# The fifth product of a channel block, taken for two blocks at once on half of the partitions each

## Chip, core and metric

The kernel runs on one core of a Trainium2 chip. The metric is the device time of one execution in microseconds (us); less is better. The core's engines are called as the profile calls them: PE is TensorE's matmul, PEld its weight load, DVE is VectorE, ACT is ScalarE, POOL is GpSimd, and SP issues DMAs. Products are summed in PSUM, of which a bank holds 128 partitions x 512 fp32.

## The reference

```
x, u: (8, 4096, 192)   w_tok1: (4096, 256)   w_tok2: (256, 4096)   w_ch1: (192, 1536)   w_ch2: (1536, 192)
x  = causal 7-tap convolution of x along the sequence; taps are the softmax of each of 8 heads' weights
h  = relu(x^T @ w_tok1) @ w_tok2          # along the sequence, per batch
u  = x + h^T
out = u + relu(u @ w_ch1) @ w_ch2         # along the channels
```

The weights come as float64 and are decoded on the core into a high and a low part.

## The kernel before

The batches are done in groups of one, one, two, two and two. A tile is 512 rows of the sequence of one batch; there are 64 tiles. While the channel part of a group runs on TensorE, VectorE and ScalarE convolve and mix the next group in the background.

A full-precision product is made of products in float32r, of which one pass takes the high part of a number and another pass the rest. `transposed()` turns a tile of u (512 rows x 192 channels) so that channels lie on partitions, and leaves three tiles of 128 x 512: `a`, the high part of channels 0 to 127; `b`, their low part; and `c`, in whose one half lie the high parts of channels 128 to 191 and in whose other half the low parts (for the first batch of a group the high parts are on partitions 0 to 63, for the second on 64 to 127).

Channel product 1 (`channel1`, with `channel1_mm`) makes 12 blocks of 128 hidden channels for each tile. A block is five products, each with 128 partitions and 512 columns, summed into one `ps_x` bank: `ah` with `a`, `al` with `a`, `ah` with `b`, `ch` with `c`, `cl` with `c`. `ch` and `cl` are the high and low parts of the last 64 rows of w_ch1, each standing twice, on the lower and on the upper 64 partitions; they are the two halves of the tile `w_c`. ScalarE then writes the relu's high part `hh`, and VectorE the rest `hl`, both from the same bank. `ps_x` has four banks, which the blocks take in turn; the transposes and mixing product 2 (`mix2`) take them too. The very first tile goes through `first_channel1`, which writes one fp32 tile in place of `hh` and `hl`.

Channel product 2 (`channel2`, lines 921 and 922) makes four sums of 12 x 2 products from `hh` and `hl`. Per tile the order on TensorE is: channel product 1, (for the last batch of a group) mixing product 2 of the next tile, one half of channel product 2, (likewise) the transposes of the next tile, the other half of channel product 2.

The order of the background work is set when the program is built, by a planner (`Background`) with two clocks, `pe` and `dve`, in ns. `bg.fg(pe, dve)` moves on TensorE's clock by the cost of a foreground step, puts background items into the queues until VectorE's clock is 600 ns past TensorE's, and then adds the step's own VectorE cost. For a block of channel product 1 the call is

```
bg.fg(1080, 700)
```

and the block's `hh` and `hl` are issued behind it, so what `fg` has put into the queues stands ahead of them. A taps item is two VectorE instructions (L624).

Of the kernel before, what the change touches and what calls it, by code (L numbers as in the profile page):

```python
# [8 lines left out]
F32 = mybir.dt.float32  # L9
F32R = mybir.dt.float32r  # L10
U32 = mybir.dt.uint32
AF = mybir.ActivationFunctionType
ALU = mybir.AluOpType
# [96 lines left out]
def conv_mixer_kernel(ctx: ExitStack, tc: tile.TileContext, x, weight, w_tok1, w_tok2, w_ch1, w_ch2, out):  # L110
    nc = tc.nc
# [5 lines left out]
    P = 128  # L117
    NJ = S // P
    KC = JT // P
    NF = FF // P  # L120
    D2 = D - P
    TJ = 4
    NT = NJ // TJ
    TT = TJ * P
# [5 lines left out]
    def f32(ap):  # L130
        return ap.bitcast(F32)
# [5 lines left out]
    ps_x = ctx.enter_context(tc.tile_pool(name="ps_x", bufs=4, space=bass.MemoryType.PSUM))  # L137
    ps_c2 = ctx.enter_context(tc.tile_pool(name="ps_c2", bufs=2, space=bass.MemoryType.PSUM))
    ps_a = ctx.enter_context(tc.tile_pool(name="ps_a", bufs=1, space=bass.MemoryType.PSUM))
    bg = Background()  # L140

    w1 = {n: const.tile([P, FF], F32R, name=f"w1_{n}") for n in ("ah", "al")}
# [682 lines left out]

    def transposed(gi, u):

        nb = len(GROUPS[gi])
        abc = [{n: (sp if i else up).tile([P, TT], F32R, name=f"{n}{i}") for n in ("a", "b", "c")} for i in range(nb)]

        rest = up.tile([P, TJ, 2, D2], F32, name="rest")
        for i in range(2):
            nc.scalar.copy(out=rest[:, :, i, :], in_=u[:, :, min(i, nb - 1), P:D])  # L833

        def cols(j, c):
            return u[:, j, c, 0:P] if c < nb else rest[:, j].rearrange("p b d -> p (b d)")

        for c in range(nb + 1):
            ps = ps_x.tile([P, TT], F32, name="ps_x")
            for j in range(TJ):  # L840
                nc.tensor.transpose(out=ps[:, j * P:(j + 1) * P], in_=cols(j, c), identity=ident)  # L841
            bg.fg(440, 600 if c < nb else 600 * nb)
            if c < nb:
                t = abc[c]
                nc.scalar.copy(out=t["a"], in_=ps)  # L845
                nc.vector.tensor_tensor(out=t["b"], in0=ps, in1=f32(t["a"]), op=ALU.subtract)
            else:
                for i in range(nb):
                    t = abc[i]["c"]
                    hs = slice(0, D2) if i == 0 else slice(D2, 2 * D2)  # L850
                    ls = slice(D2, 2 * D2) if i == 0 else slice(0, D2)
                    nc.scalar.copy(out=t[hs], in_=ps[hs])
                    nc.vector.tensor_tensor(out=t[ls], in0=ps[hs], in1=f32(t[hs]), op=ALU.subtract)  # L853
        return abc

    t2s_of(0)
    up = ctx.enter_context(tc.tile_pool(name="up", bufs=1))
    first = {}
# [12 lines left out]
    def first_transposed():  # L871
        first["abc"] = transposed(0, first["u"][1])

    def channel1_mm(t, f):
        fs = slice(f * P, (f + 1) * P)
        ps = ps_x.tile([P, TT], F32, name="ps_x")
        prods = (("ah", "a"), ("al", "a"), ("ah", "b"), ("ch", "c"), ("cl", "c"))
        for n, (w, v) in enumerate(prods):
            nc.tensor.matmul(out=ps, lhsT=w1[w][:, fs], rhs=t[v], start=n == 0, stop=n == len(prods) - 1)  # L879
        return ps  # L880


    def first_channel1(fs):
        for f in fs:
            ps = channel1_mm(first["abc"][0], f)
            bg.fg(1080, 0)
            nc.scalar.activation(out=first["h"][:, f], in_=ps, func=AF.Relu)

    def first_channel2(u, osb, js):
        for j in js:  # L890
# [9 lines left out]
    def channel1(t):  # L900
        h = {}
        for f0 in range(0, NF, NF // 3):
            for n in ("hh", "hl"):
                part = hp.tile([P, NF // 3, TT], F32R, name=f"{n}{f0}")
                for f in range(NF // 3):
                    h[n, f0 + f] = part[:, f]
        for f in range(NF):
            ps = channel1_mm(t, f)
            bg.fg(1080, 700)
            nc.scalar.activation(out=h["hh", f], in_=ps, func=AF.Relu)  # L910
            nc.vector.scalar_tensor_tensor(  # L911
                out=h["hl", f], in0=ps, scalar=0.0, in1=f32(h["hh", f]), op0=ALU.max, op1=ALU.subtract
            )
        return h

    def channel2(i, h, u, osb, js):
# [33 lines left out]
    def first_done():  # L950
# [8 lines left out]
    stage1_first(  # L959
        pe, p0, pd, first_late, first_load, first_next, first_done,  # L960
        [first_mix, first_transposed] + [lambda fs=fs: first_channel1(fs) for fs in thirds],
    )
    pd_ctx.close()
# [65 lines left out]
    for gi, bs in enumerate(GROUPS):  # L1029
        nb = len(bs)  # L1030
# [9 lines left out]
        if gi == 0:  # L1040
            u, abc = first["u"][1], first["abc"]
            loaded = first["next"]
        for q in range(NT):
            nxt = (gi, q + 1) if q + 1 < NT else (gi + 1, 0)
            for i, b in enumerate(bs):
                turn = i == nb - 1 and nxt[0] < len(GROUPS)
                run_ahead(gi)
                if turn and nxt[0] != gi:
                    starts[nxt[0]][1]()
                    if gi == 0:  # L1050
                        cp = cp or conv_pool()
                        t2s_ctx.close()
                        sp = ctx.enter_context(tc.tile_pool(name="sp1", bufs=1, reuse_waits="tile"))
# [3 lines left out]
                if ahead:  # L1057
                    h = channel1(abc[i])
                    run_ahead(gi)
                    osb = hp.tile([P, TJ, D], F32, name="osb")  # L1060
                else:
                    osb = first["osb"]
                    first_channel2(u, osb, half[0])
# [7 lines left out]
                if turn:  # L1071
                    abc = transposed(nxt[0], loaded[1])
# [50 lines left out]
```

## Time and profile before

| what | value |
|---|---|
| median of 3 runs | 2143.77 us (2142.07 to 2144.6) |
| profiled execution | 2145.54 us |
| its span, first to last instruction | 2143.6 us |
| granted TensorE clock | 0.998 |
| PE, PEld, DVE, ACT busy | 2108.9, 1948.3, 1369.2, 733.3 us |
| products of line 879 | 3840 = 64 tiles x 12 blocks x 5 |

Busy times of an engine are the union of its instructions' times. A matmul's time runs from its start to a modelled end and overlaps the next one's; what a matmul costs in a row of them is the distance between starts. In a timeline the columns are start in us, duration in us, engine, line, operation, written tile and read tiles, shape and count, and in brackets how long the engine was idle before it and what released it.

### The profile page before, as it was taken

What the parts mean: (1) busy time and instruction counts of PE and PEld (TensorE: products, weight loads), DVE (VectorE), ACT (ScalarE), POOL (GpSimd) and SP (SyncE); (2) the same over time, 40 slices, a digit from 0 to 9 for tenths busy, and PEclk for the clock granted to TensorE, in tenths of its full rate; (3) what the DMA queues carried; (4) which work ended last, traced back from release to release, by engine and by line L of the source; (5) the groups of instructions that cost most, each with busy time, mean ns of one, the idle gap of its engine ahead of it and who ended that gap; (6) DMA issues with size and microseconds to landing.
All of it is one profiled execution on the core that took longest, in us unless ns stands there. A gap on an engine that the chain in (4) does not pass through costs nothing.

```text
span 2143.6 us, 29665 instructions
## 1 busy us (share of the span) xinstructions
PE 2108.9 (98%) x12202; PEld 1948.3 (91%) x12202; DVE 1369.2 (64%) x2564; ACT 733.3 (34%) x1231; POOL 74.3 (3%) x134
## 2 busy tenths in 40 slices
PE   5999999999999999999999999999999999999999
PEld 5889999999999999999999999999999999999998
DVE  5789979888788986964445884444444444444443
ACT  3455544343433333333223332233223232223222
POOL 1100000000000000000000000000000000000000
PEclk9999999999999999999999999999999999999999
DMA  9835544554534634341112432111111111111100
GB/s 315 264 121 178 172 150 140 179 178 144 174 110 151 197 126 124 97 149 33 47 50 85 144 118 70 42 50 50 50 30 47 46 34 50 49 43 50 50 16 15
DMA packets 159175, 221.83 MB, mean 103 GB/s; under 512 B 106166, under 2 KB 116406, under 8 KB 154432
## 3 DMA queue, kind: packets, MB, share of 16 engines
q1 hardware_dynamic: 148240, 157.36, 24.3%
q0 software_dynamic: 10800, 62.58, 7.3%
q8 instruction: 96, 1.57, 0.3%
q14 instruction: 39, 0.32, 0.0%
HBM read 147.03 MB, written 71.30 MB: 102 GB/s over the span
## 4 chain that ended last, share of the span: by engine, by line
PE 94%; DVE 2%; DMA 1%; ACT 1%; issue 1%; POOL 0%; SPq 0%; ACTq 0%
PE ps_x L879 38%; PE ps_c L921 28%; PE ps_c L922 12%; PE ps_x L841 2%; PE ps_a L712 2%; PE ps_x L819 2%; PE ps_x L817 2%; PE ps_a L714 2%; PE ps_x L818 2%; PE ps_a L713 2%; PE ps_a L708 1%; PE ps_a L428 1%; PE ps_x L814 1%; DVE hl L911 1%; PE ps_x L495 1%
## 5 line engine op out<-in xcount | busy, mean ns | idle before, releaser
L921 PE MATMUL ps_c<-w,hh 128*128 128x384 f32 x3024 | 869.9, 360 | 0.0
L922 PE MATMUL ps_c<-w,hl 128*128 128x192 f32 x3024 | 757.3, 250 | 0.0
L910 ACT ACTIVATE hh<-ps_x 128x512 fp32r<-128x512 f32 x756 | 448.7, 598 | 880.8 <-PE ps_x L879 880.0
L911 DVE SCALAR_TENSOR_TENSOR hl<-ps_x,hh 128x512 fp32r<-128x512 f32 x756 | 511.9, 689 | 278.2 <-ACT hh L910 277.0
L922 PEld LDWEIGHTS ps_c<-w,hl 128*128 128x128 f32 x3024 | 578.8, 191 | 1.0
L921 PEld LDWEIGHTS ps_c<-w,hh 128*128 128x128 f32 x3024 | 567.8, 188 | 1.0
L879 PE MATMUL ps_x<-c,w_c 128*128 128x512 f32 x1536 | 474.3, 390 | 0.1
L624 DVE SCALAR_TENSOR_TENSOR xc<-raw,cw,xc 128x384 f32<-128x384 f32 (+1 forms) x768 | 386.0, 562 | 16.8 <-ACT xc L622 16.2
L879 PEld LDWEIGHTS ps_x<-c,w_c 128*128 128x128 f32 x1536 | 288.9, 188 | 61.3 <-DVE c L853 0.8
L925 DVE TENSOR_TENSOR osb<-ps_c,u 128x192 f32<-128x192 f32 x252 | 89.8, 356 | 370.1 <-PE ps_c L922 369.4
L879 PE MATMUL ps_x<-a,w_ah 128*128 128x512 f32 x768 | 303.3, 395 | 2.0 <-DVE hl L911 2.0
L879 PE MATMUL ps_x<-b,w_ah 128*128 128x512 f32 x768 | 299.8, 390 | 0.0
L879 PE MATMUL ps_x<-a,w_al 128*128 128x512 f32 x768 | 299.7, 390 | 0.0
L879 PEld LDWEIGHTS ps_x<-a,w_ah 128*128 128x128 f32 x768 | 144.6, 188 | 32.6 <-DVE hl L911 5.8
L879 PEld LDWEIGHTS ps_x<-b,w_ah 128*128 128x128 f32 x768 | 144.5, 188 | 30.4
L879 PEld LDWEIGHTS ps_x<-a,w_al 128*128 128x128 f32 x768 | 144.8, 188 | 26.6
L845 ACT CAST a<-ps_x 128x512 fp32r<-128x512 f32 x64 | 35.2, 588 | 190.7 <-PE ps_x L841 190.6
L822 DVE TENSOR_TENSOR u<-ps_x,u 128x384 f32<-128x384 f32 (+1 forms) x160 | 75.3, 472 | 32.7 <-PE ps_x L819 29.3
L926 DVE TENSOR_TENSOR osb<-ps_c,osb 128x192 f32<-128x192 f32 x252 | 90.1, 358 | 8.7
L933 POOL DMA_DIRECT2D out_dram<-osb x63 | 35.8, 568 | 1604.8 <-DVE osb L926 1583.7
L833 ACT COPY rest<-u 128x256 f32<-128x256 f32 x80 | 28.5, 403 | 119.8 <-DVE u L822 83.5
L622 ACT ACTIVATE xc<-raw,cw 128x384 f32<-128x384 f32 (+1 forms) x128 | 66.0, 568 | 0.3 <-DVE xhl L696 0.2
(110 smaller groups left out, 1499.0 us busy)
## 6 DMA issues: line engine op xcount, KB each, us to landing
raw<-in_x_dram SPq DMA_DIRECT2D x56, 672.0 KB, 8.0
t<-t2d SPq DMA_DIRECT2D x64, 512.0 KB, 4.7
out_dram<-osb POOLq DMA_DIRECT2D x63, 384.0 KB, 5.1
xcd<-xc POOLq DMA_DIRECT2D x12, 1536.0 KB, 8.4
u<-xcd SPq DMA_DIRECT2D x24, 768.0 KB, 4.8
t<-t1p SPq DMA_DIRECT2D x16, 1024.0 KB, 5.1
t2d<-stage SPq DMA_DIRECT2D x16, 512.0 KB, 2.8
t1p<-t POOLq DMA_DIRECT2D x8, 1024.0 KB, 7.4
```

Source lines behind the costliest of these rows:

```text
L622: nc.scalar.activation(out=dst, in_=src, func=AF.Copy, scale=cw[:, h, 0:1])
L624: nc.vector.scalar_tensor_tensor(out=dst, in0=src, scalar=cw[:, h, k:k + 1], in1=dst, op0=ALU.mult, op1=ALU.add)
L712: nc.tensor.matmul(out=ps, lhsT=wh, rhs=xh, start=a, stop=False)
L713: nc.tensor.matmul(out=ps, lhsT=wh, rhs=xl, start=False, stop=False)
L822: nc.vector.tensor_tensor(out=uj, in0=ps[:, :n], in1=uj, op=ALU.add)
L879: nc.tensor.matmul(out=ps, lhsT=w1[w][:, fs], rhs=t[v], start=n == 0, stop=n == len(prods) - 1)
L910: nc.scalar.activation(out=h["hh", f], in_=ps, func=AF.Relu)
L911: nc.vector.scalar_tensor_tensor(out=h["hl", f], in0=ps, scalar=0.0, in1=f32(h["hh", f]), op0=ALU.max, op1=ALU.subtract)
L921: nc.tensor.matmul(out=ps[:, :2 * D], lhsT=h["hh", f][:, ts], rhs=w2[:, f, :], start=f == 0, stop=False)
L922: nc.tensor.matmul(out=ps[:, :D], lhsT=h["hl", f][:, ts], rhs=w2[:, f, :D], start=False, stop=f == NF - 1)
L925: nc.vector.tensor_tensor(out=osb[:, j], in0=ps[:, 0:D], in1=u[:, j, i, :], op=ALU.add)
L926: nc.vector.tensor_tensor(out=osb[:, j], in0=ps[:, D:2 * D], in1=osb[:, j], op=ALU.add)
```

## The change

The blocks of channel product 1 are made in pairs, f and f + 1. The first four products of both blocks come first, the four of f and then the four of f + 1, in two banks. The fifth product of each follows: it takes only the high parts of u's last 64 channels (the low parts times `cl` are left out, a term of the size that the scheme leaves out for channels 0 to 127 as well), so it has 64 partitions. Block f takes the lower 64 partitions of `cl` and of u, block f + 1 the upper 64. So the high parts have to lie on both halves: one copy is the half of `c` that holds them, the other is a half of a new tile `e`, which ScalarE copies from the same bank behind `c`. The built program marks these products as 64 x 128 tiles at rows 0 and 64; all others of the channel products are 128 x 128. The evictions `hh` and `hl` of both blocks stand behind the pair, and the planner is called once for a pair with twice the numbers.

```diff
@@ transposed
-        abc = [{n: (sp if i else up).tile([P, TT], F32R, name=f"{n}{i}") for n in ("a", "b", "c")} for i in range(nb)]
+        abc = [{n: (sp if i else up).tile([P, TT], F32R, name=f"{n}{i}") for n in ("a", "b", "c", "e")} for i in range(nb)]
...
                     nc.scalar.copy(out=t[hs], in_=ps[hs])
                     nc.vector.tensor_tensor(out=t[ls], in0=ps[hs], in1=f32(t[hs]), op=ALU.subtract)
+                    nc.scalar.copy(out=abc[i]["e"][ls], in_=ps[hs])
+                    abc[i]["high"] = [t[hs], abc[i]["e"][ls]] if i == 0 else [abc[i]["e"][ls], t[hs]]
@@ channel1_mm
-        fs = slice(f * P, (f + 1) * P)
-        ps = ps_x.tile([P, TT], F32, name="ps_x")
-        prods = (("ah", "a"), ("al", "a"), ("ah", "b"), ("ch", "c"), ("cl", "c"))
-        for n, (w, v) in enumerate(prods):
-            nc.tensor.matmul(out=ps, lhsT=w1[w][:, fs], rhs=t[v], start=n == 0, stop=n == len(prods) - 1)
-        return ps
+        pss = []
+        for i in range(2):
+            fs = slice((f + i) * P, (f + i + 1) * P)
+            ps = ps_x.tile([P, TT], F32, name="ps_x")
+            pss.append(ps)
+            for n, (w, v) in enumerate((("ah", "a"), ("al", "a"), ("ah", "b"), ("ch", "c"))):
+                nc.tensor.matmul(out=ps, lhsT=w1[w][:, fs], rhs=t[v], start=n == 0, stop=False)
+        for i, ps in enumerate(pss):
+            fs = slice((f + i) * P, (f + i + 1) * P)
+            rows = slice(i * D2, (i + 1) * D2)
+            nc.tensor.matmul(out=ps, lhsT=w1["cl"][rows, fs], rhs=t["high"][i], start=False, stop=True)
+        return pss
@@ channel1 (first_channel1 likewise, with bg.fg(2160, 0) and the relu alone)
-        for f in range(NF):
-            ps = channel1_mm(t, f)
-            bg.fg(1080, 700)
-            nc.scalar.activation(out=h["hh", f], in_=ps, func=AF.Relu)
-            nc.vector.scalar_tensor_tensor(
-                out=h["hl", f], in0=ps, scalar=0.0, in1=f32(h["hh", f]), op0=ALU.max, op1=ALU.subtract
-            )
+        for f in range(0, NF, 2):
+            pss = channel1_mm(t, f)
+            bg.fg(2160, 1400)
+            for i, ps in enumerate(pss):
+                nc.scalar.activation(out=h["hh", f + i], in_=ps, func=AF.Relu)
+                nc.vector.scalar_tensor_tensor(
+                    out=h["hl", f + i], in0=ps, scalar=0.0, in1=f32(h["hh", f + i]), op0=ALU.max, op1=ALU.subtract
+                )
```

On TensorE the first two blocks of the second tile stand like this before (a number behind a name tells one buffer from another; `w1_c` holds `ch` and `cl`):

```order
L879 MATMUL ps_x_801<-a0_709,w1_ah_71 128x512
L879 MATMUL ps_x_801<-a0_709,w1_al_72 128x512
L879 MATMUL ps_x_801<-b0_710,w1_ah_71 128x512
L879 MATMUL ps_x_801<-c0_711,w1_c_381 128x512 x2
L879 MATMUL ps_x_814<-a0_709,w1_ah_71 128x512
```

After, the same two blocks with their ten products are:

```order
L885 MATMUL ps_x_805<-a0_711,w1_ah_71 128x512
L885 MATMUL ps_x_805<-a0_711,w1_al_72 128x512
L885 MATMUL ps_x_805<-b0_712,w1_ah_71 128x512
L885 MATMUL ps_x_805<-c0_713,w1_c_381 128x512
L885 MATMUL ps_x_810<-a0_711,w1_ah_71 128x512
L885 MATMUL ps_x_810<-a0_711,w1_al_72 128x512
L885 MATMUL ps_x_810<-b0_712,w1_ah_71 128x512
L885 MATMUL ps_x_810<-c0_713,w1_c_381 128x512
L889 MATMUL ps_x_805<-c0_713,w1_c_381 128x512
L889 MATMUL ps_x_810<-e0_714,w1_c_381 128x512
```

The last product of the first block has moved behind four of the second, and the two 64-row products (L889; their output is still 128 x 512) stand next to each other. On VectorE, in the channel product 1 of the third tile, the evictions `hl` (line 911) and the background before:

```order
L911 SCALAR_TENSOR_TENSOR hl_1124<-ps_x,hh_1123 128x512
L624 SCALAR_TENSOR_TENSOR xc<-raw_649,cw,xc 128x8x24 x2
L911 SCALAR_TENSOR_TENSOR hl_1124<-ps_x,hh_1123 128x512 x2
L624 SCALAR_TENSOR_TENSOR xc<-raw_649,cw,xc 128x8x24 x2
L911 SCALAR_TENSOR_TENSOR hl_1124<-ps_x,hh_1123 128x512
```

and after (the eviction is line 923 there):

```order
L624 SCALAR_TENSOR_TENSOR xc<-raw_651,cw,xc 128x8x24 x4
L923 SCALAR_TENSOR_TENSOR hl_1130<-ps_x,hh_1129 128x512 x2
L624 SCALAR_TENSOR_TENSOR xc<-raw_651,cw,xc 128x8x24 x4
L923 SCALAR_TENSOR_TENSOR hl_1130<-ps_x,hh_1129 128x512 x2
L161 TENSOR_SCALAR dec_top<-dec_top 128x512
```

Evictions stand by twos, and up to four background instructions ahead of two of them where it was two ahead of one or two.

More of the change, by code (lines that the diff above doesn't have):

```diff
@@ L874, in channel1_mm @@
     def channel1_mm(t, f):
-        fs = slice(f * P, (f + 1) * P)
-        ps = ps_x.tile([P, TT], F32, name="ps_x")
-        prods = (("ah", "a"), ("al", "a"), ("ah", "b"), ("ch", "c"), ("cl", "c"))
-        for n, (w, v) in enumerate(prods):
-            nc.tensor.matmul(out=ps, lhsT=w1[w][:, fs], rhs=t[v], start=n == 0, stop=n == len(prods) - 1)
-        return ps
-    def first_channel1(fs):
[L884 to L887, printed above, removed]
+        pss = []
[10 more added lines that the diff above has]
+        return pss
+    def first_channel1(fs):
+        for f in fs[::2]:
+            pss = channel1_mm(first["abc"][0], f)
+            bg.fg(2160, 0)
+            for i, ps in enumerate(pss):
+                nc.scalar.activation(out=first["h"][:, f + i], in_=ps, func=AF.Relu)
     def first_channel2(u, osb, js):
@@ L906, in channel1 @@
                     h[n, f0 + f] = part[:, f]
-        for f in range(NF):
-            ps = channel1_mm(t, f)
-            bg.fg(1080, 700)
-            nc.scalar.activation(out=h["hh", f], in_=ps, func=AF.Relu)
-            nc.vector.scalar_tensor_tensor(
-                out=h["hl", f], in0=ps, scalar=0.0, in1=f32(h["hh", f]), op0=ALU.max, op1=ALU.subtract
-            )
+        for f in range(0, NF, 2):
+            pss = channel1_mm(t, f)
+            bg.fg(2160, 1400)
+            for i, ps in enumerate(pss):
+                nc.scalar.activation(out=h["hh", f + i], in_=ps, func=AF.Relu)
+                nc.vector.scalar_tensor_tensor(
+                    out=h["hl", f + i], in0=ps, scalar=0.0, in1=f32(h["hh", f + i]), op0=ALU.max, op1=ALU.subtract
+                )
         return h
```

## The prediction

> **What bounds the kernel now.** The first part of the page, the chain of work that ended last and the groups were read first.
>
> ```profile
> span 2143.6 us, 29665 instructions
> PE 2108.9 (98%) x12202; PEld 1948.3 (91%) x12202; DVE 1369.2 (64%) x2564; ACT 733.3 (34%) x1231; POOL 74.3 (3%) x134
> PE 94%; DVE 2%; DMA 1%; ACT 1%; issue 1%; POOL 0%; SPq 0%; ACTq 0%
> PE ps_x L879 38%; PE ps_c L921 28%; PE ps_c L922 12%; PE ps_x L841 2%; PE ps_a L712 2%; PE ps_x L819 2%; PE ps_x L817 2%; PE ps_a L714 2%; PE ps_x L818 2%; PE ps_a L713 2%; PE ps_a L708 1%; PE ps_a L428 1%; PE ps_x L814 1%; DVE hl L911 1%; PE ps_x L495 1%
> L879 PE MATMUL ps_x<-c,w_c 128*128 128x512 f32 x1536 | 474.3, 390 | 0.1
> L910 ACT ACTIVATE hh<-ps_x 128x512 fp32r<-128x512 f32 x756 | 448.7, 598 | 880.8 <-PE ps_x L879 880.0
> L911 DVE SCALAR_TENSOR_TENSOR hl<-ps_x,hh 128x512 fp32r<-128x512 f32 x756 | 511.9, 689 | 278.2 <-ACT hh L910 277.0
> ```
>
> TensorE is the chain: 94% of it, and 38% is the line that the change rewrites. The 1536 products of c are two for each of 768 blocks. So time saved on TensorE is saved in the end, unless a new wait takes it. The 390 ns is one product from start to end, not its price: the price is read from starts. The timeline of a quiet stretch, matmuls and weight loads:
>
> ```profile
> 1513.46 0.39 PE L879 MATMUL ps_x<-c,w_c 128*128 128x512 f32 x1
> 1513.69 0.39 PE L879 MATMUL ps_x<-a,w_ah 128*128 128x512 f32 x1
> 1513.69 0.19 PEld L879 LDWEIGHTS ps_x<-a,w_al 128*128 128x128 f32 x1
> 1513.92 0.39 PE L879 MATMUL ps_x<-a,w_al 128*128 128x512 f32 x1
> 1513.92 0.19 PEld L879 LDWEIGHTS ps_x<-b,w_ah 128*128 128x128 f32 x1
> 1514.82 0.39 PE L879 MATMUL ps_x<-a,w_ah 128*128 128x512 f32 x1
> 1527.04 0.34 PE L819 MATMUL ps_x<-h,t 128*128 128x384 f32 x1
> 1529.13 0.33 PE L819 MATMUL ps_x<-h,t 128*128 128x384 f32 x1
> ```
>
> A block (five products, 1513.69 to 1514.82) takes 1.133 us, so a product takes 0.227. The 384-wide products take 2.09/12 = 0.174; the 128 columns between them are worth 0.053, so 512 columns stream in about 0.213 and some 0.013 is fixed. The remaining 0.39 − 0.213 = 0.176 is latency behind the last column. Each weight load starts when the matmul before its own starts, never sooner.
>
> **The change, part by part.**
>
> *The two halves.* Per pair of blocks, ten slots of 0.227 become eight and one slot of two 64-row products. No trace row has two products on different rows at once, so that slot is bounded. Upper end: they run one behind the other, 0.453, no gain. Lower end: the second starts the fixed 0.013 behind the first, 0.240, a gain of 0.213. Between lies the weight load: if the second half's load starts, as every load above, when the matmul before it starts, its product follows one load later. Channel product 2, whose 192-wide product is too short to cover a load, shows what that costs:
>
> ```profile
> 1499.93 0.25 PE L922 MATMUL ps_c<-w,hl 128*128 128x192 f32 x1
> 1500.02 0.36 PE L921 MATMUL ps_c<-w,hh 128*128 128x384 f32 x1
> 1499.93 0.19 PEld L921 LDWEIGHTS ps_c<-w,hh 128*128 128x128 f32 x1
> 1500.04 0.19 PEld L922 LDWEIGHTS ps_c<-w,hl 128*128 128x128 f32 x1
> ```
>
> Load at 1499.93, product at 1500.02: 0.09. The slot is then 0.09 + 0.227 = 0.317, a gain of 0.137. I take this one, since it needs no load earlier than those rows have. 64 tiles × 6 pairs = 384 pairs: −52.6 us (ends −81.8 and 0).
>
> *Changing the form.* Per pair the array goes from 128-row to 64-row products and back. The nearest rows with a change of form are the transposes, entered from 128-row matmuls and left to them:
>
> ```profile
> 1537.06 0.25 PE L922 MATMUL ps_c<-w,hl 128*128 128x192 f32 x1
> 1537.15 1.03 PE L841 MATMUL ps_x<-ident,u 128*128 128x128 f32 x8
> 1538.38 0.42 PE L921 MATMUL ps_c<-w,hh 128*128 128x384 f32 x1
> 1538.63 0.25 PE L922 MATMUL ps_c<-w,hl 128*128 128x192 f32 x1
> 1512.53 0.42 PE L879 MATMUL ps_x<-a,w_ah 128*128 128x512 f32 x1
> 1512.79 0.39 PE L879 MATMUL ps_x<-a,w_al 128*128 128x512 f32 x1
> ```
>
> In: 0.09 after the product before, as without a change. Out: the next product follows after 0.25; but 0.26 instead of 0.227 also follows the plain change of tile at 1512.53, which changes no form. So I take 0 for a change. The other end is that each has to wait out the latency, 0.176, twice a pair: 0.352 × 384 = +135 us, more if the loads wait too (rivals).
>
> *Banks come free in pairs.* Both evictions now start when the pair ends, and a pair takes two of the four ps_x banks. The quiet stretch:
>
> ```profile
> 1513.89 0.60 ACT L910 ACTIVATE hh<-ps_x 128x512 fp32r<-128x512 f32 x1 [14.19 <-PE ps_x L879]
> 1514.52 0.69 DVE L911 SCALAR_TENSOR_TENSOR hl<-ps_x,hh 128x512 fp32r<-128x512 f32 x1 [1.04 <-ACT hh L910]
> ```
>
> The block that began its last product at 1513.46 ends at 1513.85, and its bank is free at 1515.21, 1.36 later. Before, that bank is wanted three blocks on: 3 × 1.133 − 0.176 = 3.22 after the end, a slack of 1.86. After, the first bank is wanted one pair on, 2.266 − 0.137 − 0.176 = 1.95 after the end: slack 0.59. The second is free at 1.36 + 0.69 = 2.05 and wanted 0.91 later than the first, slack 0.81. So quiet stages pay nothing. In the busy ones VectorE works for the next group in between:
>
> ```profile
> 90.00:860.00 770.00, 764.61 (x4452) 707.11 (x4451) 654.34 (x1314) 319.28 (x524) 32.52 (x56) 1.00 0.48 154
> 1150.00:1300.00 150.00, 149.81 (x861) 139.62 (x860) 113.33 (x197) 52.33 (x83) 3.24 (x6) 1.00 0.38 131
> 1300.00:2143.60 843.60, 839.81 (x4875) 774.19 (x4874) 378.51 (x672) 239.20 (x417) 15.13 (x28) 1.00 0.13 41
> 637.55 0.60 ACT L910 ACTIVATE hh<-ps_x 128x512 fp32r<-128x512 f32 x1 [5.60 <-PE ps_x L879]
> 638.39 1.14 DVE L624 SCALAR_TENSOR_TENSOR xc<-raw,cw,xc 128x384 f32<-128x384 f32 x2
> 639.45 1.88 DVE L911 SCALAR_TENSOR_TENSOR hl<-ps_x,hh 128x512 fp32r<-128x512 f32 x3
> PE ps_x L879 <- DVE hl L911: 2.0, 5, 0.8
> ```
>
> VectorE (third figure) is busy 85% and 76% there, 45% behind 1300. The eviction that could start at 638.15 starts at 639.45, 1.3 late: inside the old slack, 0.7 beyond the new. Today all such waits cost 2.0 us. By share of TensorE's time (920 of 2143.6 us) some 160 pairs lie there; lower end 0, upper end one two-tap item (1.14) ahead of every pair, 160 × (1.14 − 0.59) = 88 us. VectorE still has room on average, and a wait of one pair gives the next its time back, so I take 0.1 a pair: +16 us. The planner deepens this a little: told 2160 ns per pair, it lets about two items stand together ahead of two evictions, where one stood ahead of each.
>
> *The new copy e.* 64 times one or two ScalarE copies like that of c, 0.58 us:
>
> ```profile
> L852 ACT CAST c<-ps_x 64x512 fp32r<-64x512 f32 x64 | 37.3, 583 | 30.2 <-DVE c L853 29.5 <-PE ps_x L841 0.7
> 628.18 1.31 PE ps_x L841 x12
> 636.29 3.44 PE ps_x L879 x15
> ```
>
> 37 us more on an engine that is busy 34%. Behind the transposes (628.18) stands half a channel product 2 before the next channel product 1 (636.29): 8.1 us that cover one or two copies; e itself is read last in its pair. Zero; if the cover went, at most 2 × 0.58 once a tile.
>
> *The end of channel product 1.* Product 2 needs the last hl only 11 × 0.285 us after it starts; the last eviction ends 2.05 behind the pair: zero when quiet, in the 16 us when busy. The left-out low part of u times the low part of the weight costs nothing: it rode along.
>
> Sum: −52.6 + 0 + 16 = −37 us. The profiled execution took 2145.5 (span 2143.6 and 1.9 around it), 1.8 above the median 2143.77; against the median the forecast is 2106 us.
>
> **Rivals.**
>
> *Each change of form waits* (slower). The pair then costs −0.213 + 2 × 0.176 = +0.139 if the loads still go ahead: +53 us, with the 16 us 2213. If the loads wait as well, 2 × (0.176 + 0.09) − 0.213 = +0.319: +122 us, 2266. It decides from 0.107 us per change with the halves fully together, 0.068 with the staggered load. For it: the transposes change form, but not the number of rows, so they don't exclude it. Against it: nothing in the rows waits out the 0.176 where a form changes. TensorEngine Tiling (Array Packing) of the Trainium skill, section Key Properties, says that changing the tiling mode drains TensorE, and gives no price. No run here shows it yet.
>
> *Both loads go ahead, the halves run together.* −81.8 + 16, 2078; without the eviction waits 2062. For it: the second half uses rows that the first doesn't, so its load has no weights of its own rows to wait for. Against: no load above goes two matmuls ahead. TensorE: Matmul & The Clock Gate of the Trainium skill, section Part 3: Packing small matmuls, says that products on different row groups start about 4 ns apart; by that the slot would be 0.231 and the time this rival's. The trace has no such pair.
>
> *The halves don't overlap.* Nothing saved, 16 us of waits: 2160, or 2144 without them. The trace neither supports nor excludes it.
>
> *VectorE becomes the bound in the busy stages:* the 88 us end, −52.6 + 88, 2179. Against: 76 to 85% busy there.
>
> **How the numbers follow.** Halves staggered by one load, or together with a small price for the change: 0.32 (2090 to 2138). Fully together: 0.22 (2062 to 2090). Changes of form that wait: 0.30 (2140 to 2270). No overlap: 0.10. VectorE: 0.06. The first two are faster, 0.54. Of the last three, 0.46, some end within 0.2% (4.3 us, about what a measurement of this kernel can tell from no change): 0.04 of the changes of form at a price between the ends, 0.02 of no overlap without waits; slower is the rest, 0.40. The range 2064 to 2230 leaves out about 0.03 below and 0.10 above; both signs being likely, the forecast's own range is 2078 to 2135.
>
> **What would show it.** Per pair in a quiet stretch, 2.13 us from first product to first product (now 2.266); the two halves' starts 0.09 apart, and the next load at the second's start. Starts 0.01 apart and 2.05 a pair speak for the second rival, a gap of over 0.2 ahead of or behind the halves for the first, starts 0.227 apart for the third. Waits of TensorE for hl near 16 us, all before 860 and in 1150 to 1300; above 60, VectorE binds. The forecast is wrong if a change of rows costs more than 0.07 us.

## The result: slower by 4.5%, and where the time went

The changed kernel takes 2239.46 us (2237.98 to 2240.46) against 2143.8 us before, a ratio of 1.0447 (95% interval [1.0429, 1.0465]; the brackets below are of the same kind); the profiled execution has a span of 2238.6 us. The forecast was 2106 us, with a range up to 2230. The first part of its page:

```profile
span 2238.6 us, 29725 instructions
PE 2192.6 (98%) x12202; PEld 1849.0 (83%) x12202; DVE 1346.8 (60%) x2564; ACT 735.8 (33%) x1295; POOL 74.6 (3%) x134
```

TensorE reads busier (2192.6 for 2108.9) with the same 12202 matmuls, of which two in each pair now stream at the same time. So its busy share says nothing of what was saved; the rows to read are the starts. One pair's end in a quiet stretch, matmuls and weight loads (lines 885 and 889 are the 128-row and the 64-row products):

```profile
1582.38 0.39 PE L885 MATMUL ps_x<-c,w_c 128*128 128x512 f32 x1
1582.70 0.18 PEld L889 LDWEIGHTS ps_x<-e,w_c 64*128 64x128 f32 x1 [0.36 <-issue]
1582.70 0.49 PE L889 MATMUL ps_x<-e,w_c 64*128 64x512 f32 x1
1582.70 0.18 PEld L889 LDWEIGHTS ps_x<-c,w_c 64*128 64x128 f32 x1
1582.70 0.49 PE L889 MATMUL ps_x<-c,w_c 64*128 64x512 f32 x1
1583.12 0.19 PEld L885 LDWEIGHTS ps_x<-a,w_ah 128*128 128x128 f32 x1 [0.24 <-issue]
1583.12 0.50 PE L885 MATMUL ps_x<-a,w_ah 128*128 128x512 f32 x1
1583.46 0.40 PE L885 MATMUL ps_x<-a,w_al 128*128 128x512 f32 x1
1583.70 0.40 PE L885 MATMUL ps_x<-b,w_ah 128*128 128x512 f32 x1
```

The two halves start together, at 1582.70. But their weight loads start there too, 0.32 us behind the product before, where the loads of the kernel before started with it (1513.69 and 1513.92 in the prediction's rows). The same at the way out: the load for the next 128-row product starts at 1583.12, 0.42 behind the halves, and the product after that follows 0.34 later. From the last c product (1582.38) to the second product behind the halves (1583.46) is 1.08 us; before, those four steps took 4 × 0.227 = 0.91. Two or three further products come about 0.235 apart. Starts of the same product in successive pairs of one tile are 2.471 us apart in the median (302 of them, from the trace), 2.267 before: +0.204, times 384 pairs +78 us. The waits of TensorE and of its weight loads on the sequencer:

```profile
PE ps_x L885 <- DVE hl L923: 13.9, 13, 5.1
PEld ps_x L889 <- issue: 137.9, 384, 0.7
PEld ps_x L885 <- issue: 66.0, 268, 0.4
```

"Issue" is time in which an engine waited for nothing that the profile shows: 384 visits, each with the weight path idle going in. The waits for banks went from 2.0 to 13.9 us (+12). 78 + 12 = 90 of the 95 us. Two stretches at waits for `hl` (1.64 us, ended at 124.14, and 5.14 us, ended at 200.99) had a granted clock of 0.50, half of full speed (third figure from the end); the kernel before had 1.00 over the same windows:

```profile
125.00:128.40 3.40, 3.40 (x9) 1.97 (x8) 2.47 (x6) 2.76 (x3) 0.00 (x0) 0.50 0.81 321
200.10:206.90 6.80, 5.91 (x14) 3.95 (x15) 4.62 (x10) 1.08 (x2) 0.00 (x0) 0.50 0.71 247
```

Half of 10.2 us is up to 5 us more (an estimate). The experiments part the loss by another way.

### The profile page after: what moved, and what is told of

Same layout as the page of the kernel before. It is cut to its first block, busy times and chain, and to the rows that moved or that the text cites. A ratio compares the mean times of both kernels' runs of the same rounds, so it can differ in the third digit from the quotient of the medians.

```text
span 2238.6 us, 29725 instructions
## 1 busy us (share of the span) xinstructions
PE 2192.6 (98%) x12202; PEld 1849.0 (83%) x12202; DVE 1346.8 (60%) x2564; ACT 735.8 (33%) x1295; POOL 74.6 (3%) x134
## 4 chain that ended last, share of the span: by engine, by line
PE 88%; DVE 7%; ACT 2%; DMA 1%; issue 1%; POOL 0%; SPq 0%; ACTq 0%; DVEq 0%; POOLq 0%
PE ps_x L885 31%; PE ps_c L933 24%; PE ps_c L934 11%; PE ps_x L889 7%; DVE xc L624 3%; PE ps_x L842 2%; PE ps_x L817 2%; PE ps_a L712 2%; PE ps_a L714 1%; PE ps_a L713 1%; PE ps_x L818 1%; PE ps_x L819 1%; DVE hl L923 1%; PE ps_a L428 1%; ACT hh L922 1%
## 5 line engine op out<-in xcount | busy, mean ns | idle before, releaser
L923 DVE SCALAR_TENSOR_TENSOR hl<-ps_x,hh 128x512 fp32r<-128x512 f32 x756 | 485.8, 685 | 384.9 <-ACT hh L922 382.7
L922 ACT ACTIVATE hh<-ps_x 128x512 fp32r<-128x512 f32 x756 | 410.8, 596 | 917.4 <-PE ps_x L889 917.3
L624 DVE SCALAR_TENSOR_TENSOR xc<-raw,cw,xc 128x384 f32<-128x384 f32 (+1 forms) x768 | 385.3, 560 | 24.9 <-ACT xc L622 24.4
L885 PE MATMUL ps_x<-a,w_ah 128*128 128x512 f32 x768 | 339.1, 442 | 13.9 <-DVE hl L923 13.9
L885 PE MATMUL ps_x<-c,w_c 128*128 128x512 f32 x768 | 302.7, 394 | 0.1
L889 PE MATMUL ps_x<-c,w_c 64*128 64x512 f32 x384 | 192.1, 500 | 0.0
L889 PE MATMUL ps_x<-e,w_c 64*128 64x512 f32 x384 | 192.0, 500 | 0.0
L885 PEld LDWEIGHTS ps_x<-c,w_c 128*128 128x128 f32 x768 | 145.0, 189 | 34.2 <-DVE c L854 0.8
L889 PEld LDWEIGHTS ps_x<-c,w_c 64*128 64x128 f32 x384 | 70.5, 184 | 86.0 <-issue 86.0
L889 PEld LDWEIGHTS ps_x<-e,w_c 64*128 64x128 f32 x384 | 70.4, 183 | 52.0 <-issue 52.0
```

Source lines behind the costliest of these rows:

```text
L624: nc.vector.scalar_tensor_tensor(out=dst, in0=src, scalar=cw[:, h, k:k + 1], in1=dst, op0=ALU.mult, op1=ALU.add)
L889: nc.tensor.matmul(out=ps, lhsT=w1["cl"][rows, fs], rhs=t["high"][i], start=False, stop=True)
L922: nc.scalar.activation(out=h["hh", f + i], in_=ps, func=AF.Relu)
L923: nc.vector.scalar_tensor_tensor(out=h["hl", f + i], in0=ps, scalar=0.0, in1=f32(h["hh", f + i]), op0=ALU.max, op1=ALU.subtract)
```

## Experiments

A visit is what a sequence of 64-row products between two 128-row products is called below. Theory A: TensorE's array changes between 128-row and 64-row products only when it has run empty, and the loads wait for that, so each visit has a price of some 0.42 us whatever is in it (the 0.204 that a pair lost and the 0.213 that its overlap saved). Rival B: the order by pairs, the planner and the evictions cost most of it. Rival C: two 64-row products side by side stream at half speed (their 0.42 us would be just two times 0.213).

### Pairs with 128-row products

```diff
-            nc.tensor.matmul(out=ps, lhsT=w1["cl"][rows, fs], rhs=t["high"][i], start=False, stop=True)
+            nc.tensor.matmul(out=ps, lhsT=w1["cl"][:, fs], rhs=t["c"], start=False, stop=True)
```

> The pairs, their order, the copy e, the planner's doubled numbers and the evictions by twos stay as in the changed kernel; only the fifth products take 128 rows again (c with cl). Theory A (the loss is the price of changing between 128-row and 64-row products, 0.42 us for going in and out): no change of rows is left, so a pair takes 2.267 us in a quiet stretch and only the waits for banks remain, about 12 us: 2156 us (2145 to 2165). Rival B (the order by pairs, the planner or the evictions cost most of the 96 us): it stays over 2200. Rival C (two 64-row products side by side run at half speed): like A here.

Measured 2172.13 us, 1.0131 [1.0116, 1.0146]. The pair's step is back at 2.267 us in the median, so the 64 rows made it longer, and 67 of the 96 us went with them: B falls as the main cause. But pairing alone costs 28 us, more than the 12 expected and above A's range. TensorE's waits and the longest one:

```profile
PE ps_x L885 <- DVE hl L923: 16.0, 13, 5.3
...
192.18 0.61 PE L889 MATMUL ps_x<-c,w_c 128*128 128x512 f32 x2
198.09 0.80 PE L885 MATMUL ps_x<-a,w_ah 128*128 128x512 f32 x1 [5.30 <-DVE hl L923]
198.68 0.63 PE L885 MATMUL ps_x<-a,w_al 128*128 128x512 f32 x1
199.11 0.63 PE L885 MATMUL ps_x<-b,w_ah 128*128 128x512 f32 x1
...
202.08 0.40 PE L885 MATMUL ps_x<-a,w_ah 128*128 128x512 f32 x1
```

### Both halves on the lower rows

```diff
+            nc.tensor.matmul(out=ps, lhsT=w1["cl"][0:D2, fs], rhs=t["high"][0], start=False, stop=True)
```

> Both fifth products of a pair take the lower 64 rows (weights and high parts), so they can't run side by side; all else as in the changed kernel. Theory A (rows change: 0.42 us per visit; side by side the halves share one slot): the slot is lost again, 384 x 0.213 = +82 us on 2239: 2321 us, starts of the halves about 0.227 apart. Rival C (no price of that size for changing; side by side each half streams at half speed, 0.43 us for both): one behind the other they run at full speed, 2 x 0.227 = 0.454 in place of 0.43, so 2239 + 9 = 2248 us.

Measured 2312.91 us, 1.0793 [1.0777, 1.0809]. The timeline shows the two in one row:

```profile
1699.49 0.39 PE L885 MATMUL ps_x<-c,w_c 128*128 128x512 f32 x1
1699.81 0.73 PE L889 MATMUL ps_x<-e,w_c 64*128 64x512 f32 x2
1700.46 0.50 PE L885 MATMUL ps_x<-a,w_ah 128*128 128x512 f32 x1
1700.80 0.40 PE L885 MATMUL ps_x<-a,w_al 128*128 128x512 f32 x1
```

0.65 us for the halves in place of 0.42: a second slot costs about 0.23. The kernel takes 73 us more than the changed one, so side by side that slot was saved, and C (2248) falls.

### Each fifth product by itself

The fifth product of a block stands directly behind its own four, with 64 rows, lower for even and upper for odd blocks; planner and evictions as before.

```diff
...
+        rows = slice(f % 2 * D2, (f % 2 + 1) * D2)
+        nc.tensor.matmul(out=ps, lhsT=w1["cl"][rows, fs], rhs=t["high"][f % 2], start=False, stop=True)
```

> Blocks one at a time in the order, with the planner's calls and evictions of the kernel before; the fifth product of each block has 64 rows, on the lower half for even and the upper for odd blocks, directly behind its own four. Twice as many visits to 64 rows as in the changed kernel, none with two products side by side. Theory A (0.42 us per visit): 768 x 0.43 = +330 us on 2144: 2474 us. Rival C (half speed only side by side; what is left of the price, 0.09 going in and 0.14 behind, per visit): 768 x 0.23 = +177: 2320 us. If 64-row products had no price when alone: 2144.

Measured 2456.18 us, 1.1462 [1.1444, 1.1479]: +312 us, 0.41 per visit. A single half takes the same way as two did:

```profile
1699.80 0.39 PE L881 MATMUL ps_x<-c,w_c 128*128 128x512 f32 x1
1700.12 0.49 PE L883 MATMUL ps_x<-c,w_c 64*128 64x512 f32 x1
1700.54 0.50 PE L881 MATMUL ps_x<-a,w_ah 128*128 128x512 f32 x1
1700.88 0.40 PE L881 MATMUL ps_x<-a,w_al 128*128 128x512 f32 x1
```

0.32, 0.42, 0.34, together 1.08, as in the changed kernel with two halves: the price belongs to the visit, not to the pair of halves.

### Halves of two pairs next to each other

In every other pair the 64-row products come first.

```diff
+        first = f % 4 == 2
...
+        if first:
+            halves()
```

> In every other pair the two 64-row products come first instead of last, so those of two pairs stand next to each other: 3 visits per tile in place of 6, each with two slots of halves. Theory A (price per visit, 0.42 us, gain 0.213 per slot): per two pairs 0.42 - 0.43, about nothing, so 2144 plus waits for banks as in the changed kernel, 2144 to 2165. Rival C (half speed side by side): a slot of halves costs 0.43 wherever it stands, and 0.23 per visit: +0.19 us per two pairs, 192 x 0.19 = +36: 2180 plus the same waits.

Measured 2178.99 us, 1.0168 [1.0151, 1.0185]. That is above A's 2144 to 2165 and just under C's 2180, so the time alone does not decide. The pairs with 128 rows, which have the same grouping, show that the waits were set too low, as there; against them it is 7 us more, where A wants about nothing and C 36. What the 7 us are was not sought. The rows decide: one visit (each slot's second half, which starts within 0.01 us of the first, is left out):

```profile
1700.88 0.39 PE L893 MATMUL ps_x<-c,w_c 128*128 128x512 f32 x1
1701.20 0.49 PE L886 MATMUL ps_x<-c,w_c 64*128 64x512 f32 x1
...
1701.53 0.39 PE L886 MATMUL ps_x<-c,w_c 64*128 64x512 f32 x1
...
1701.86 0.50 PE L893 MATMUL ps_x<-a,w_ah 128*128 128x512 f32 x1
1702.20 0.39 PE L893 MATMUL ps_x<-a,w_al 128*128 128x512 f32 x1
```

1.32 us from c to al, where six 128-row steps took 1.36 and C asks for 1.55 (1.36 + 0.19).

### Three slots a visit

If the price is per visit, three slots in one visit must win. Six blocks are open at once, in the four ps_x and the two ps_c2 banks: two get their four 128-row products, the visit completes these two and opens four others, whose 128-row products follow. The first tile is done as in the kernel before.

```diff
+        for i in range(2):
+            pss.append(ps_c2.tile([P, TT], F32, name="ps_c2"))
+            four(pss[i], f + i, True)
+        bg.fg(1730, 0)
+        for i in range(6):
...
+            nc.tensor.matmul(
+                out=pss[i], lhsT=w1["cl"][rows, fs], rhs=t["high"][i % 2], start=i > 1, stop=i < 2
+            )
```

> Six blocks share a visit: two blocks get their first four products in the two ps_c2 banks (idle in channel product 1), then six 64-row products in three slots complete these two and open four blocks in the ps_x banks, whose four 128-row products follow; evictions one by one, planner's numbers 1730, 1090 with 1400, and 865 with 700. The first tile is done as in the kernel before. Theory A (0.42 us per visit, 0.213 saved per slot): 126 visits x (0.42 - 0.64) = -28 us, plus waits for banks of 0 to 20 us: 2116 to 2136 us, below both kernels. Rival C (half speed side by side, 0.23 per visit, no gain per slot but 0.454 - 0.43): 126 x (0.23 - 0.07) = +20: 2164 us plus waits.

Measured 2169.76 us (2157.52 to 2173.32), 1.0129 [1.0112, 1.0146]: not below. The trace is of the fastest execution, 2157.52 us, with a granted clock of 0.997; over the two slowest, near 2173, it was 0.989 (by an estimate, 0.008 × 2170 = 17 us, about the spread), and what held it down there is in no trace. Its waits name a new one, the ps_c2 bank that the tile before has not given back:

```profile
PE ps_c L888 <- DVE osb L959: 26.7, 21, 3.3
```

Turned round, so that the opening blocks lie in ps_x and the ps_c2 banks are taken last in the visit and finished first:

```diff
+        banks = [ps_x, ps_x, ps_c2, ps_c2, ps_x, ps_x]
...
+        for i in (0, 1, 4, 5, 2, 3):
```

> As the kernel with three slots a visit, but the two blocks that open a group lie in ps_x banks, and the two ps_c2 banks are taken last in the visit and completed first behind it: they are first wanted 2.2 us after a tile's start in place of 0 and 0.9. If the 27 us that TensorE waited there for the osb of the tile before (DVE osb) are what kept that kernel over the one before: 2170 - 20 to 27 = 2143 to 2150 us, and if the other executions of it (2157) are typical, 2130 to 2137. If the price of a visit is higher than 0.42 us or VectorE is simply late in the busy stages, the waits move to ps_x: 2155 to 2170.

Measured 2119.88 us (2119.82 to 2120.73), 0.9889 [0.9876, 0.9903]: 24 us below the kernel before, inside the 2116 to 2136 that theory A gave for three slots, and the version to keep. The turned order gave more than the 20 to 27 us expected: 50 between the medians, 37.7 between the traced executions (2157.5 and 2119.8). The wait rows count idle time alone, so they show less than the starts: in the trace of the first order the first products of blocks come 36 us later, in sum, than 0.227 behind the product ahead of them, and in that of the turned one 1.1 us. A visit, and what is left of the wait:

```profile
1707.98 0.39 PE L888 MATMUL ps_x<-c,w_c 128*128 128x512 f32 x1
1708.30 0.49 PE L907 MATMUL ps_x<-c,w_c 64*128 64x512 f32 x1
...
1708.63 0.39 PE L907 MATMUL ps_x<-c,w_c 64*128 64x512 f32 x1
...
1708.87 0.39 PE L907 MATMUL ps_c<-c,w_c 64*128 64x512 f32 x1
...
1709.19 0.50 PE L888 MATMUL ps_c<-a,w_ah 128*128 128x512 f32 x1
1709.53 0.40 PE L888 MATMUL ps_c<-a,w_al 128*128 128x512 f32 x1
...
PE ps_c L907 <- DVE osb L964: 3.5, 4, 1.5
```

1.55 us where eight steps took 1.82. The four stretches from c to al, each against the steps that it replaces, make the rule (the products behind a visit, some 0.03 late, are not in it):

| halves in a visit | stretch | steps replaced | difference |
|---|---|---|---|
| one | 1.08 | 3 × 0.227 = 0.68 | +0.40 |
| two side by side | 1.08 | 4 × 0.227 = 0.91 | +0.17 |
| two times two | 1.32 | 6 × 0.227 = 1.36 | −0.04 |
| three times two | 1.55 | 8 × 0.227 = 1.82 | −0.27 |

A slot more costs 0.23 to 0.24 and saves two steps of 0.227.

### What pairing itself costs

With the banks turned and less background work let ahead of the evictions (`bg.fg(..., 0)` in place of 600):

> As the one with the banks turned, and in channel product 1 the planner lets VectorE's clock stand 0 instead of 600 ns past TensorE's, so less background work stands ahead of the evictions. If late evictions cost the rest: 5 to 15 us below the one with the banks turned, 2125 to 2140. If the background work is then missing later (the next group's mix not ready): no gain, or slower by some 10 us.

Measured 2138.13 us, 0.9973 [0.9962, 0.9983]: 18 us worse than with 600. That is the second expectation's case by its size; its reason is not shown. The trace shows a wait for osb of 10.8 us (from 3.5) and a granted clock of 0.996 (from 0.999). The planner's 600 is no loss there. For the 28 us of the pairs with 128 rows, the planner was called by block:

```diff
-            bg.fg(2160, 1400)
             for i, ps in enumerate(pss):
+                bg.fg(1080, 700)
```

> Pairs with 128-row fifth products as in the first experiment, but the planner is called once for each block of the pair (1080, 700), ahead of that block's eviction, as in the kernel before. If the 28 us that pairing alone costs come from the planner's doubled step (two items ahead of two evictions): 2150 to 2160 us. If they come from the evictions starting only at the pair's end: 2165 to 2175.

Measured 2163.88 us, 1.0092 [1.0079, 1.0106], between the two cases. Then, apart from it, each block's five products in a row, planned and evicted by pairs:

> 128-row products, each block's five in a row as in the kernel before; planner and evictions by pairs as in the changed kernel. Pairing with 128 rows cost 28 us, 8 of which went when the planner was called by block. If the other 20 come from the first block's fifth product standing behind the second block's four, so that its eviction starts 0.9 us later: 2148 to 2154 us here. If they come from issuing evictions and background by twos: 2165 to 2172.

Measured 2164.21 us, 1.0094 [1.0078, 1.0111], 1 us below the second case. And both undone, the copy e kept:

> 128-row products in each block's own order and the planner called by block: of the change only the copy e is left (and a second bank taken a little earlier in the program's text, not in TensorE's order). If the copy is free, as predicted: 2142 to 2148 us, and the 28 us of pairing alone lie in the two things undone here together. If ScalarE's copies delay evictions or transposes: 2150 to 2160.

Measured 2147.77 us, 1.0019 [1.0009, 1.0029]. So what is left costs about 4 us. It is not the copy alone: background products of TensorE, which stood behind any block before (5, 15, 45 or 55 products of channel product 1 in a row in the trace), stand behind pairs alone here (10, 20, 30, 40 or 50), against what was expected. The late fifth product alone adds 16 (2163.9 − 2147.8), the doubled planner step alone 16 (2164.2 − 2147.8), both together 24 (2172.1 − 2147.8): they don't add up. TensorE's waits for `hl` in the three runs above, in their order, against 2.0 in the kernel before and 16.0 in the pairs with 128 rows:

```profile
PE ps_x L885 <- DVE hl L923: 9.5, 14, 2.1
PE ps_x L886 <- DVE hl L920: 15.9, 13, 5.0
PE ps_x L886 <- DVE hl L920: 4.5, 6, 2.1
```

That both use up the same slack of the banks is the likely reading; no run shows it by itself.

## The prediction, step by step

- **What bounds the kernel**: right. TensorE's starts decide; what lengthened them lengthened the kernel.
- **The two halves**: too careful. They start together (the second rival's row), not one load apart: within a visit both loads go at once. With both on one half the kernel lost 73 us, 0.191 a pair, near the 0.213 of full overlap. By the rows there it is 0.65 − 0.42 = 0.23. So the overlap gained about 0.2 a pair, not the 0.137 taken.
- **Changing the form**: the step that failed. A change between 128-row and 64-row products was taken at 0 from the transposes, which change the form of the product but keep all 128 rows. Measured, going in costs 0.32 − 0.227 = 0.09, and coming out 0.42 − 0.24 = 0.18, then 0.34 − 0.227 = 0.11 and some 0.03 in the products behind: 0.41 a visit. In the visit with two slots (1700.88 to 1702.20) the rows part it: steps of 0.32, 0.33, 0.33 and 0.34 in place of 0.227, so each of the two changes delays the first product behind it by about 0.1 and the one after that by about 0.1. The row that was needed was not in the trace: its one change in the number of rows, from 38-row to 128-row products at 27.09, stands behind a wait for ScalarE (0.65 us) and shows no price. The other end, 2 × 0.176 = 0.352, was nearer, and loads that wait as well (0.53) a little too far. TensorEngine Tiling (Array Packing) of the Trainium skill, section Key Properties, which was quoted for the first rival, says that a change of tiling mode drains TensorE. The trace agrees, with a shorter wait than the 0.176 taken for it: the next load starts 0.32 behind the product before, 0.107 after the estimated 0.213 of streaming.
- **The first rival**: +0.139 to +0.319 a pair, 2213 to 2266 us (the 2266 leaves out the 16 us of waits; with them it is 2282); measured +0.204 and 2239. Its mechanism is the one that the runs show, in the form in which the loads wait as well. It had a chance of 0.30, and the range, which ended at 2230, took in only its lower part.
- **Banks that come free in pairs**: 16 us forecast; 13.9 us of waits in the changed kernel, 24 us for the whole pairing (2172.1 − 2147.8). That 13.9 came near 16 is luck: 0.1 us at each of 160 pairs was forecast, and 13 waits were measured, one of them 5.1 us, twelve of them before 860 and none in 1150 to 1300. The cause is broader too: the late product and the doubled planner step, which was to deepen it a little, add 16 each, and some of the long waits bring a half clock with them.
- **The copy e**: forecast 0; together with the moved background products it measured 4 us (0.19% [0.09, 0.29]). The forecast counted the copy's own 0.58 us. In that run ScalarE also waits 72.2 us, in 64 waits, for VectorE's part of c before it copies e. Which of these makes the 4 us was not tried.
- **Third and last rival**: halves that don't overlap, and VectorE as the bound, are excluded by the starts at 1582.70 and by the 13.9 us of waits for `hl`, where the prediction had set 60 as the sign.
- **The sum**: 2143.77 − 36.6 is 2107, not 2106; nothing hangs on it. Taken off one after another, the 95.7 us are 67.3 of the 64 rows (2239.5 − 2172.1), 24.4 of the pairing (2172.1 − 2147.8) and 4.0 of what is left. The 78 of the result's rows is higher than the 67, in part because 75 of the 384 visits are followed by other products than another pair and lose about 0.18 each in place of 0.20.

## What to carry to other kernels

A product that needs only half of the rows saves nothing by itself: a visit to 64-row products costs 0.41 us here, and each slot of two side by side gives back 0.21, so two slots come out even and three in one visit win. That needs more open banks, and whose banks are taken first decides whether the gain survives (2169.8 or 2119.9 us for the same products). When a trace has no row for the very change that is made, the far end of the bound deserves the weight, not the nearest look-alike.

## What was not expected of the hardware

After a wait of 5.3 us (rows at 198.09 above) the 512-column products come 0.43 us apart instead of 0.227 until about 201.5, and the granted clock of that stretch is 0.50:

```profile
198.10:201.50 3.40, 3.40 (x8) 2.76 (x9) 2.99 (x6) 0.00 (x0) 0.00 (x0) 0.50 0.92 319
```

The eight steps from 198.09 to 201.61 take 3.52 us where 1.82 is usual, so this wait costs some 1.7 us more than it lasts. TensorE: Matmul & The Clock Gate of the Trainium skill, section Part 1, says that an idle window of about 3.4 us halves TensorE's clock until it has been busy as long. The trace agrees in the half and in the 3.4 us that it lasts. It differs in what brings it about: in the changed kernel a wait of 1.64 us, ended at 124.14, was enough for 0.50 from 125.0 to 128.4, while behind one of 1.76 us, ended at 747.97, the clock stayed at 1.00.

In a visit, the loads of the second slot start ahead of its products; in these traces only the change of rows holds a load back like that. The kernel with three slots a visit, loads and the second slot's product:

```profile
1710.20 0.18 PEld L902 LDWEIGHTS ps_c<-e,w_c 64*128 64x128 f32 x1 [0.36 <-issue]
...
1710.31 0.19 PEld L902 LDWEIGHTS ps_x<-e,w_c 64*128 64x128 f32 x1
...
1710.54 0.39 PE L902 MATMUL ps_x<-e,w_c 64*128 64x512 f32 x1
```

The second slot's load (1710.31) starts 0.23 us before its product (1710.54).
